# A gated mix of windowed attention and a ReGLU block with all its gradients: load order, a third unit of lag, one tensor for four gradients and outputs, and operand tiles for the first output group

## The chip, the cores and the metric

The kernel runs on one core of one Trainium2 chip. A core has TensorE (PE, the matrix products, with PEld as its weight loads), VectorE (DVE), ScalarE (ACT), GpSimd (POOL) and SyncE (SP), which here only issues DMAs. SP and ACT issue DMAs on queues of their own, and POOL on a third. The metric is the device time of one execution in microseconds (us), as the median of several runs. All engines run in program order and wait for each other by semaphores, so an instruction that waits holds up all that stand behind it on its engine.

## The reference

With x of 2048 rows and 512 columns in bf16, the forward part is

```
q, k, v = split(x @ wqkv)                  # 32 heads of 16
p = softmax(q k^T / 4, causal, window 256)
a = (p v) @ wo
b = (relu(x @ W_gate) * (x @ W_up)) @ W_down        # 1376 hidden columns
g = sigmoid(sum(x * gate_w))               # one number per row
out = g * a + (1 - g) * b
```

The kernel returns `out` and, for a given `grad_out`, the gradients of x, wqkv, wo, W_gate, W_up, W_down and gate_w: eight outputs in all.

## The kernel before

The names are those of the code. Rows come in 16 tiles of 128 (index t or j), which make 4 groups of 512 (TPG = 4 tiles, index tg); the 512 model columns are 4 chunks c of 128, that is 8 heads each; the 1376 hidden columns are 11 chunks fc.

**First loads (L143 to L163).** SP loads x for the first group, then the other three groups, then the first chunk of W_down (`Wd_sb`) and its rest. ACT's queue loads the first 256 columns of W_gate and W_up (`W0`), the gate vector as columns, and later the rest of both weights (L159, L160). POOL's queue loads grad_out by groups into `go_in`, which has two buffers: the third and fourth load are asked for in `db_rows` after the first and second group have been used.

**Feed-forward (L321 to L365).** A loop of steps n, one for each (fc, tg) pair, 44 in all. In step n the kernel does the gate and up products of pair n, in the first four steps also the transposes of x (`turn_x`), the gate column (`gate_col`), the rows (1-g)*grad_out (`db_rows`, on DVE) and one step later their transposes (`turn_db`). With a lag of 1 come the product `dh` and a DMA transpose of hT (`turn_h`), of 2 the DMA transpose of dgT, of 3 the transposes of duT on PE and the stores of hT, dgT and duT to DRAM (`keep`, on ACT's queue), of 4 the weight gradients (`weights`). Between them lie the rows g*grad_out (da), the zeroing of a DRAM scratch, and the load of wqkv and the transposed load of wo.

**Attention (L385 to L850).** `project_parts(c, tg)` makes Q, dO, K and V transposed for one chunk and group, then their rows. `spread` writes Q and dO to a DRAM scratch, `gather` reads them back in a block-diagonal tile `zt` (two of them, for two tiles j each), so that one product does four heads. A unit is (c, j, kb, half): one tile of queries, one of keys, four heads; there are 360, of role "d" (kb = j), "m" and "f". The hand-written order of one iteration n is: small POOL work that is due; `front` of unit n (ST and dPT on PE, exp on ACT, the mask on POOL); `gradp` of unit n-1 (DVE: Pd = Pu * dPT); `rowsum` and `flip` of unit n-2; one or two pieces of the CD products (the sums that give dK and dV); then background pieces (projections of the next group, or weight gradients of the chunk before, `grad_parts`); last the DMAs that are due. `flip` transposes Pu and Pd: for role "d" by a DMA on SP, for the others on PE with a copy on ACT or DVE in turn. `small_ops` divides by the row sums in five later iterations. PSUM has four banks of tag M (ST, dPT, projections and weight gradients), two of tag TR (transposes), one for CD and one for BA (row sums).

dQ, dK, dV (`dqkv_st`) and O (`O_st`) of a chunk stay in SBUF and are written by `spill`, half of the rows at a time, with four DMAs to two DRAM tensors: `dqkv_d`, where a row piece is 128 columns or 256 bytes, and `O_d`. The last half of the last chunk goes by POOL's queue.

During the last chunk `late_weights` (L478) loads the weights of the output stage on SP: wo, the transposed wqkv, W_gate and W_up from DRAM copies, and W_down, 5.9 MB, once the projections of the last group are done. `early_group` (L693) brings da rows and, from tile 12 on, the transposed dqkv and O of the first 256 rows. Behind the loop come `load_group(0)`, the 20 pieces of weight gradients of the last chunk, and their stores on SP from a tile `ws` with two buffers.

**Output stage (L872 to L934).** Eight groups of two tiles; while a group is computed the next is loaded on SP. A tile takes 11 products for b (`bps`), 4 for a (`aps`), the evictions and the gate's gradient dz on ACT, DVE and POOL, then 34 products for dx (`dxps`): the chunks of dgT and duT in turn, then 12 with dqT. The gate vector's gradient (`dgw_ps`) of a tile is added one tile later, and that of the last tile after everything else; its copy is on DVE. dx goes out on POOL's queue.

Of the kernel before, what the change touches and what calls it, by code (L numbers as in the profile page):

```python
# [22 lines left out]
def kernel(  # L23
# [64 lines left out]
    dqkv_d = dram.tile([S, 3 * D], BF, name="dqkv_d")  # L88
    O_d = dram.tile([S, D], BF, name="O_d")
# [33 lines left out]
    with ExitStack() as p1, tc.manual_schedule():  # L123
# [25 lines left out]
        nc.sync.dma_start(x_r[:, 0:TPG, :], rows_of(x_d, 0))  # L149
# [4 lines left out]
        load_go(0)  # L154
        load_go(1)
# [3 lines left out]
        nc.scalar.dma_start(Wg_sb[:, :, W0:F], Wg_v[:, :, W0:F])  # L159
        nc.scalar.dma_start(Wu_sb[:, :, W0:F], Wu_v[:, :, W0:F])  # L160
# [24 lines left out]
        def db_rows(tg):  # L185
            for k in range(TPG):
                t = tg * TPG + k
                nc.vector.tensor_scalar(db_r[:, t, :], go_in[tg][:, k, :], omg_all[:, t:t + 1], None, op0=ALU.mult)
            if tg + 2 < NTG:
                load_go(tg + 2)  # L190
# [81 lines left out]
        def turn_h(k):  # L272
            k.h_r = fp.tile([P, TPG, P], BF, tag="h_r", name="h_r")
            nc.sync.dma_start_transpose(out=k.h_r[:], in_=k.hT[:])
# [11 lines left out]
        def keep(k):  # L286
            for dst, src in ((hT_d, k.hT), (dgT_d, k.dgT), (duT_d, k.duT)):
                nc.scalar.dma_start(dst[k.fsl, k.ts], src[:])
# [31 lines left out]
        for n in range(N1 + 6):  # L320
# [16 lines left out]
            if at(2):  # L337
                turn_dg(at(2))
            if at(3):
                turn_du(at(3))  # L340
                keep(at(3))
            if at(4):
                f = weights(at(4))
# [24 lines left out]
    if True:  # L368
        st = p3.enter_context(tc.tile_pool(name="attst", bufs=2))
        gwp = p3.enter_context(tc.tile_pool(name="gwp", bufs=2))  # L370
        p3b = ExitStack()
        wq = p3b.enter_context(tc.tile_pool(name="wq", bufs=1))
# [3 lines left out]
        zt = [wq.tile([P, 2, HG, 2 * P], BF, name=f"z{i}") for i in range(ZB)]  # L376
# [8 lines left out]
        def project_parts(c, tg):  # L385
# [32 lines left out]
            def tr_kv():  # L418
# [3 lines left out]
                for a, lo, eng in ((0, 0, "dve"), (1, 17, "dve")):  # L422
# [3 lines left out]
            return [lambda: mm("Q", 0, "dve"), lambda: mm("dO", 3, "dve"), lambda: mm("K", 1, "dve"),  # L426
                    lambda: mm("V", 2, "dve"), tr_rows, tr_kv]
# [18 lines left out]
        def cd_piece(c, kb, qb, half, last):  # L446
# [12 lines left out]
            if last:  # L459
                nc.scalar.copy(sts[c][0][:, kb, 1:3, :].rearrange("p a (h d) -> p h a d", h=HG),  # L460
# [4 lines left out]
        def spill(c, t0):  # L465
            dqkv_st, O_st = sts[c]
            tsl = slice(t0, t0 + NT // 2)
            rsl = slice(t0 * P, (t0 + NT // 2) * P)
# [40 lines left out]
        def grad_parts(c, rest=None):  # L509
# [22 lines left out]
            def piece(part, t0, first, last):  # L532
                dqkv_st, O_st = sts[c]
                if first:
                    hold["w"] = ps.tile([P, 3, P] if part < DC else [P, D], F32, tag="M", bufs=4, name="wps")
                wps = hold["w"]
                for t in range(t0, t0 + 4):
                    go_, no_ = first and t == t0, last and t == t0 + 3
                    if part < DC:
                        nc.tensor.matmul(wps[:], lhsT=x_r[:, t, part * P:(part + 1) * P], rhs=dqkv_st[:, t, :, :],  # L540
                                         start=go_, stop=no_)
                    else:
                        nc.tensor.matmul(wps[:], lhsT=O_st[:, t, :], rhs=rows[t], start=go_, stop=no_)
                if not last:
                    return None
                if part < DC:
                    ws = gwp.tile([P, 3, P], BF, tag="ws", name="ws")
                    evac(ws[:], wps[:], "act")
# [7 lines left out]
                ws = gwp.tile([P, D], BF, tag="ws", name="ws")  # L556
# [8 lines left out]
            else:  # L565
                parts = [(p, 0, NT) for p in range(DC)] + [(DC, 0, NT)]
# [9 lines left out]
        for c in range(DC):  # L576
            for j in range(NT):
                kbs = [k for k in (j - 1, j, j - 2) if k >= 0]
                for half in range(2):
                    for ki, kb in enumerate(kbs):  # L580
# [4 lines left out]
                        u.role = ("d", "m", "f")[j - kb]  # L585
                        units.append(u)
        NU = len(units)

        def front(u):
            tg, jl = u.j // TPG, u.j % TPG  # L590
            zb = (jl // 2) % ZB
            KTt, VTt = proj[(u.c, u.kb // TPG)]["K"], proj[(u.c, u.kb // TPG)]["V"]
# [4 lines left out]
            u.dPT = ps.tile([P, HH, P], F32, tag="M", bufs=4, name="dPT")  # L597
            nc.tensor.matmul(u.dPT[:], lhsT=VTt[:, ksl], rhs=zt[zb][:, 1, hsl, (jl % 2) * P:(jl % 2 + 1) * P], start=True, stop=True)  # L598
# [3 lines left out]
            else:  # L602
                u.Pu = wk.tile([P, HH, P], BF, tag="Pu", bufs=3, name="Pu")
# [7 lines left out]

        def gradp(u):
            if u.role != "d":
                u.Pd = wk.tile([P, HH, P], BF, tag="Pd", bufs=3, name="Pd")
# [20 lines left out]
        def flip(u):  # L635
            if u.role == "d":
# [11 lines left out]
            p2 = wk.tile([P, 2, HH, P], BF, tag=f"P2{u.role}", bufs={"m": 6, "f": 4}[u.role], name="p2")  # L648
# [3 lines left out]
        def small_ops(c, j, s):  # L652
            rows = proj[(c, j // TPG)]["rows"]
            jl = j % TPG
            dqkv_st, O_st = sts[c]
# [18 lines left out]
            def pool2():  # L674
                nc.gpsimd.tensor_tensor(out=rq[:, :, Dh:2 * Dh], in0=hd(rows[:, 1, jl, :]),
                                        in1=bc(rinv[:], Dh), op=ALU.mult)
                nc.gpsimd.tensor_tensor(out=hd(O_st[:, j, :]), in0=BAs[:, :, 17:33], in1=bc(rinv[:], Dh), op=ALU.mult)
# [287 lines left out]
```

## Time and profile before

| | us |
|---|---|
| median of 3 runs | 1039.25 |
| lowest and highest | 1038.76, 1042.58 |
| the profiled execution | 1040.05 |
| its span in the profile | 1038.3 |
| PE busy | 982.8 (95%) |
| DVE busy | 569.8 (55%) |
| ACT busy | 481.1 (46%) |
| POOL busy | 466.4 (45%) |

The span is the profiled part of that one execution; 1.75 us lie around it. Busy time is the time in which an engine had an instruction of the kind that the profile counts; matmuls overlap and their ends are modelled, so the spacing of their starts says more than their durations. "PEclk" is the TensorE clock that was granted, in tenths. In the chain of waits each piece is the work or transfer that released the next one; a row reads start, length, what. In the timeline a row reads start, length, engine, line, operation, operands, count, and in brackets the idle time before it with what ended it. "SPq" and "ACTq" are the issuing of DMAs on these engines.

### The profile page before, as it was taken

To read this page: it belongs to the slowest core of one execution; us is meant where nothing else is said; L and a number is where in the kernel's file an instruction comes from. 1 tells how busy PE (TensorE), PEld (TensorE's weight loads), DVE (VectorE), ACT (ScalarE), POOL (GpSimd) and SP (SyncE) were. 2 spreads that over 40 slices of the span, in tenths; PEclk is the share of its full clock that TensorE was granted. 3 is DMA by queue.
4 is the path that set the end of the run, shared out by engine and by line. 5 is a ranking of instruction groups with operands and counts; after the bars stand their busy time and mean duration, and the time that the engine had idled before them with its cause. 6 is when DMAs were issued, how large, how long until landed. Compare 5 with 4: busy or idle time off the path is not lost.

```text
span 1038.3 us, 28954 instructions
## 1 busy us (share of the span) xinstructions
PE 982.8 (95%) x11852; PEld 634.0 (61%) x11852; DVE 569.8 (55%) x1101; ACT 481.1 (46%) x808; POOL 466.4 (45%) x810
## 2 busy tenths in 40 slices
PE   5799999999989999999999999999999769999997
PEld 3466666566647777677776777766777534444443
DVE  3344444333268888767788677886777502322222
ACT  3323333222147777666677676666667411001000
POOL 2355544344345556655556455565555411211211
PEclk9999999999999999999999999999999879999999
DMA  9557676866555676787767776569869989667740
GB/s 303 90 148 178 179 178 169 205 160 142 136 114 102 123 145 117 154 168 149 143 119 149 163 161 127 132 118 177 143 97 231 266 222 260 158 154 179 187 107 21
DMA packets 393335, 162.85 MB, mean 157 GB/s; under 512 B 293297, under 2 KB 388818, under 8 KB 393202
## 3 DMA queue, kind: packets, MB, share of 16 engines
q1 hardware_dynamic: 368306, 131.30, 60.6%
q10 hardware_dynamic: 21648, 20.13, 6.2%
q0 software_dynamic: 3248, 9.57, 3.0%
q8 instruction: 93, 1.52, 0.6%
q14 instruction: 40, 0.33, 0.1%
HBM read 54.36 MB, written 48.10 MB: 99 GB/s over the span
## 4 chain that ended last, share of the span: by engine, by line
PE 82%; DMA 7%; issue 3%; DVE 3%; ACT 2%; SPq 1%; POOL 1%; ACTq 0%; POOLq 0%; DVEq 0%
PE pt L647 9%; PE wps L298 7%; PE dPT L598 7%; PE ST L596 7%; PE gps L247 4%; PE bps L883 4%; PE dhps L247 4%; PE CD L454 4%; PE dxps L919 3%; PE BA L624 3%; PE dps L300 3%; PE pp L395 3%; PE ups L247 3%; PE dxps L912 3%; PE dxps L915 3%; PE wps L540 3%
## 5 line engine op out<-in xcount | busy, mean ns | idle before, releaser
L615 DVE TENSOR_TENSOR Pd<-Pu,dPT 128x512 bf16<-128x512 bf16 x232 | 158.3, 684 | 55.2 <-POOL Pu L609 34.1
L604 ACT ACTIVATE Pu<-ST 128x512 bf16<-128x512 f32 x232 | 139.5, 601 | 59.2 <-PE ST L596 53.2
L606 POOL TENSOR_SCALAR_AFFINE_SELECT PP<-PP 128x512 bf16<-128x512 bf16 x128 | 81.1, 634 | 160.7 <-ACT PP L604 160.1
L598 PE MATMUL dPT<-z,VT 128*128 128x512 bf16 x360 | 136.5, 379 | 4.1 <-DVE Pd L615 1.6
L596 PE MATMUL ST<-z,KT 128*128 128x512 bf16 x360 | 136.3, 379 | 0.8 <-DMA z<-z_d 0.8
L75 ACT COPY p<-pt 128x1024 bf16<-128x1024 bf16 x116 | 117.4, 1012 | 30.7 <-PE pt L647 30.3
L454 PE MATMUL CD<-rq,p 128*128 128x32 bf16 x1440 | 117.0, 177 | 7.9 <-DMA p<-PP 6.4
L457 PE MATMUL CD<-rq,p 128*128 128x16 bf16 x1440 | 113.7, 169 | 0.0
L261 POOL TENSOR_TENSOR hT<-rg,upm 128x512 bf16<-128x512 bf16 x44 | 50.5, 1148 | 134.5 <-DVE upm L259 114.0
L298 PE MATMUL wps<-dgu_r,x_r 128*128 128x256 bf16 x704 | 106.8, 275 | 2.1 <-DVE wst L77 2.0
L604 ACT ACTIVATE PP<-ST 128x512 bf16<-128x512 f32 x128 | 76.7, 600 | 55.0 <-PE ST L596 48.2
L454 PEld LDWEIGHTS <-p 128*128 128x128 bf16 x1440 | 95.8, 96 | 6.7 <-DMA p<-PP 6.7
L609 POOL TENSOR_SCALAR_AFFINE_SELECT Pu<-Pu 128x512 bf16<-128x512 bf16 x112 | 71.1, 634 | 56.3 <-ACT Pu L604 54.7
L77 DVE COPY p<-pt 128x1024 bf16<-128x1024 bf16 x116 | 79.7, 687 | 28.3 <-PE pt L647 26.8
L615 DVE TENSOR_TENSOR PP<-PP,dPT 128x512 bf16<-128x512 bf16 x128 | 86.6, 677 | 9.9 <-POOL PP L606 9.8
L624 PEld LDWEIGHTS <-Pu 128*128 128x128 bf16 x928 | 68.0, 96 | 37.3 <-issue 10.3
L647 PE MATMUL pt<-ident,Pd 128*128 128x128 bf16 x928 | 90.2, 220 | 0.0
L457 PEld LDWEIGHTS <-p 128*128 128x128 bf16 x1440 | 89.0, 96 | 1.7 <-issue 1.7
L647 PE MATMUL pt<-ident,Pu 128*128 128x128 bf16 x928 | 89.3, 218 | 0.0
L298 PEld LDWEIGHTS <-x_r 128*128 128x128 bf16 x704 | 67.6, 99 | 24.4 <-issue 3.2
L259 DVE SCALAR_TENSOR_TENSOR upm<-rg,ups 128x512 bf16<-128x512 bf16 x44 | 30.2, 687 | 94.0 <-PE ups L247 91.9
L624 PE MATMUL BA<-KV,Pu 128*128 128x33 bf16 x928 | 77.5, 178 | 4.5 <-ACT BAs L630 3.9
(136 smaller groups left out, 2073.8 us busy)
## 6 DMA issues: line engine op xcount, KB each, us to landing
z<-z_d SPq DMA_DIRECT2D x128, 64.0 KB
dar<-da_d SPq DMA_DIRECT2D x28, 256.0 KB
hT_d<-hT ACTq DMA_DIRECT2D x44, 128.0 KB
dgT_d<-dgT ACTq DMA_DIRECT2D x44, 128.0 KB
duT_d<-duT ACTq DMA_DIRECT2D x44, 128.0 KB
dqkv_d<-dqkv_st SPq DMA_DIRECT2D x21, 256.0 KB
hT_g<-hT_d SPq DMA_DIRECT2D x8, 640.0 KB
dgT_g<-dgT_d SPq DMA_DIRECT2D x8, 640.0 KB
```

The costliest lines, as they stand in the source:

```text
L75: nc.scalar.copy(out, in_)
L247: nc.tensor.matmul(out[:], lhsT=w(c), rhs=x(c), start=(c == 0), stop=(c == DC - 1))
L298: nc.tensor.matmul(acc["w"][:, c, :], lhsT=x_r[:, t, c * P:(c + 1) * P], rhs=k.dgu_r[:, :, i, :], start=(go_ and c % 2 == 0), stop=no_, sk ...
L454: nc.tensor.matmul(cd[0][:, h, :], lhsT=p2[:, 0, hh, :], rhs=rq[:, h, 0:2 * Dh], start=cd[1], stop=True, skip_group_check=True)
L457: nc.tensor.matmul(cd[0][:, h, 0:Dh], lhsT=p2[:, 1, hh, :], rhs=rq[:, h, 2 * Dh:3 * Dh], start=False, stop=True, skip_group_check=True)
L596: nc.tensor.matmul(ST[:], lhsT=KTt[:, ksl], rhs=zt[zb][:, 0, hsl, (jl % 2) * P:(jl % 2 + 1) * P], start=True, stop=True)
L598: nc.tensor.matmul(u.dPT[:], lhsT=VTt[:, ksl], rhs=zt[zb][:, 1, hsl, (jl % 2) * P:(jl % 2 + 1) * P], start=True, stop=True)
L604: nc.scalar.activation(u.Pu[:], ST[:], ACT.Exp, scale=scale)
L606: nc.gpsimd.affine_select(out=u.Pu[:], in_=u.Pu[:], compare_op=ALU.is_ge, fill=0.0, base=0, pattern=[[0, HH], [1, P]], channel_multiplier=-1)
L615: nc.vector.tensor_tensor(out=u.Pd[:], in0=u.Pu[:], in1=u.dPT[:], op=ALU.mult)
L624: nc.tensor.matmul(BA[:, h, 0:33], lhsT=u.Pu[:, hh, :], rhs=kv[:, u.kb % TPG, h, :], start=(u.first and hh == 0), stop=True, skip_group_ch ...
L647: nc.tensor.transpose(pt[:, a, hh, :], src[:, hh, :], ident[:])
```

## The change

*First loads.* x of the first group comes in two halves. go_in has four buffers and all four loads are asked for at the start. The rest of W_gate and W_up moves from ACT's queue to SP's, behind x and the first chunk of W_down and ahead of its rest. A sigmoid on one zeroed column is put at the front of ACT's work. Every second row of `db_rows` goes to ACT. `dh` runs two steps behind instead of one, `turn_dg` three, `turn_du` four, `weights` five; `keep` stores hT at a lag of 3 and the other two at 4. `h_r` has six buffers.

*Attention.* `rowsum` and the flips on PE run three units behind (LAG), the DMA flips still two. `front` is split: ST and the exp stay, dPT moves to `front_dp`, behind the row sums and flips. Pu and Pd outside the diagonal have four buffers, P2m five. K and V are copied by ACT. In the prelude the first spreads and gathers are written ahead of K and V.

*One tensor.* dQ, dK, dV and O lie side by side in one SBUF tile `rows_st` and one DRAM tensor `dqkvo_d`, by chunk, so that a spill is one DMA with runs of 1 KB and a group's transposed load is one DMA.

*End of attention.* The last projections are due 10 iterations sooner, and `late_weights` with them. The diagonal units of the last two tiles of the last chunk are flipped on PE. hT and dgT of the first output group are loaded into the two `zt` tiles when their last readers are done, and the first group's transposes start from tile 11. Of the last chunk's weight gradients, 12 pieces are done two at a time in the last iterations, in four M banks; then come four for wo's gradient and the last four. `ws` has five buffers there, and its copies alternate between ACT and DVE. The tiles of later groups share `rows_st`.

*Output stage.* dxps takes all chunks of dgT, then all of duT, then dq. In the last tile both dgw products come ahead of the dq products, the copy is on ACT, and the last dx goes out on SP.

```diff
-            go_in[tg] = fp.tile([P, TPG, D], BF, tag="go_in", bufs=2, name="go_in")
+            go_in[tg] = fp.tile([P, TPG, D], BF, tag="go_in", bufs=NTG, name="go_in")
...
+        half = TPG // 2
+        for i in range(2):
+            nc.sync.dma_start(x_r[:, i * half:(i + 1) * half, :], rows_of(x_d, 0)[:, i * half:(i + 1) * half, :])
...
+        nc.vector.memset(g_all[:, 0:1], 0.0)
+        nc.scalar.activation(g_all[:, 0:1], g_all[:, 0:1], ACT.Sigmoid)
...
-        nc.scalar.dma_start(Wg_sb[:, :, W0:F], Wg_v[:, :, W0:F])
-        nc.scalar.dma_start(Wu_sb[:, :, W0:F], Wu_v[:, :, W0:F])
+        nc.sync.dma_start(Wg_sb[:, :, W0:F], Wg_v[:, :, W0:F])
+        nc.sync.dma_start(Wu_sb[:, :, W0:F], Wu_v[:, :, W0:F])
...
+                if k % 2:
+                    nc.scalar.mul(db_r[:, t, :], go_in[tg][:, k, :], omg_all[:, t:t + 1])
...
+            if at(2):
+                dh(at(2))
             if at(1):
-                dh(at(1))
                 turn_h(at(1))
...
-            for a in range(3):
-                eng.dma_start(dqkv_d[rsl, a * D + c * P:a * D + (c + 1) * P].rearrange("(t p) n -> p t n", p=P),
-                                  dqkv_st[:, tsl, a, :])
-            eng.dma_start(O_d[rsl, c * P:(c + 1) * P].rearrange("(t p) n -> p t n", p=P), O_st[:, tsl, :])
+            eng.dma_start(dqkvo_d[t0 * P:(t0 + NT // 2) * P, c * 4 * P:(c + 1) * 4 * P].rearrange("(t p) n -> p t n", p=P),
+                          sts[c][:, tsl, :, :].rearrange("p t a n -> p t (a n)"))
...
-                parts = [(p, 0, NT) for p in range(DC)] + [(DC, 0, NT)]
+                for a, b in ((0, NT - 4), (NT - 4, NT)):
+                    if a:
+                        out += [(DC, t0, t0 == 0, t0 + 4 == NT) for t0 in range(0, NT, 4)]
+                    out += [(p, t0, t0 == 0, t0 + 4 == NT) for p in range(DC) for t0 in range(a, b, 4)]
+                return [lambda a=a: piece(*a) for a in out]
...
+                        u.dma = u.role == "d" and (c < DC - 1 or j < NT - 2)
...
+        def early_f(i):
+            flat = wq.tile([P, 2, HG, 2 * P], BF, tag=f"z{i}", name=f"f{i}")[:].rearrange("p a h q -> p (a h q)")
+            S2[f"f{i}"] = flat[:, 0:FC * GT * P].rearrange("p (c s) -> p c s", c=FC)
+            load_f(S2[f"f{i}"], (hT_d, dgT_d)[i], slice(0, GT * P))
...
+                            if gi + 2 == len(groups):
+                                due -= 10
...
-                if 2 <= n < NU + 2:
-                    w = units[n - 2]
+                if 2 <= n < NU + 2 and units[n - 2].dma:
+                    flip(units[n - 2])
+                if LAG <= n < NU + LAG:
+                    w = units[n - LAG]
                     rowsum(w)
-                    flip(w)
+                    if not w.dma:
+                        flip(w)
...
+                if u is not None:
+                    front_dp(u)
...
+                    elif n > NU + 1:
+                        for _ in range(2):
+                            if len(S2["grads"]) > 4 + DC:
+                                S2["grads"].pop(0)()
```

More of the change, by code (lines that the diff above doesn't have):

```diff
@@ L284, in turn_du, with keep @@
             evac(k.dgu_r[:, 1, :, :], pt[:], "dve")
-        def keep(k):
-            for dst, src in ((hT_d, k.hT), (dgT_d, k.dgT), (duT_d, k.duT)):
+        def keep(k, *pairs):
+            for dst, src in pairs:
                 nc.scalar.dma_start(dst[k.fsl, k.ts], src[:])
@@ L319 @@
         stores = {}
-        for n in range(N1 + 6):
+        for n in range(N1 + 7):
             at = lambda lag: steps[n - lag] if 0 <= n - lag < N1 else None
@@ L375 @@
         ZB = 2
-        zt = [wq.tile([P, 2, HG, 2 * P], BF, name=f"z{i}") for i in range(ZB)]
+        zt = [wq.tile([P, 2, HG, 2 * P], BF, tag=f"z{i}", name=f"z{i}") for i in range(ZB)]
         for i in range(ZB):
@@ L532, in piece @@
             def piece(part, t0, first, last):
-                dqkv_st, O_st = sts[c]
                 if first:
-                    hold["w"] = ps.tile([P, 3, P] if part < DC else [P, D], F32, tag="M", bufs=4, name="wps")
-                wps = hold["w"]
+                    tag, bufs = ("TR", 2) if part == DC and rest is not None else ("M", 4)
+                    hold[part] = ps.tile([P, 3, P] if part < DC else [P, D], F32, tag=tag, bufs=bufs, name="wps")
+                wps = hold[part]
                 for t in range(t0, t0 + 4):
@@ L734, in load_group @@
-            return hT_g, dgT_g, duT_g, dqT_g, go_g, OT_g
+                T_g, hT_g, dgT_g = S2["T0"], S2["f0"], S2["f1"]
+                go_g = S2["g6"].tile([P, GT, D], BF, tag="go_g", bufs=1)
+            else:
+                flat = st.tile([P, NT, 4, P], BF, tag="rows_st", name="gt")[:].rearrange("p t a n -> p (t a n)")
+                n1, n2 = 4 * DC * GT * P, (4 * DC + FC) * GT * P
+                T_g = flat[:, 0:n1].rearrange("p (c s) -> p c s", c=4 * DC)
+                hT_g = flat[:, n1:n2].rearrange("p (c s) -> p c s", c=FC)
+                go_g = flat[:, n2:n2 + GT * D].rearrange("p (t d) -> p t d", t=GT)
+                dgT_g = S2["g6"].tile([P, FC, GT * P], BF, tag="dgT_g")
+                load_f(hT_g, hT_d, gsl)
@@ L736 @@
+            duT_g = S2["g6"].tile([P, FC, GT * P], BF, tag="duT_g")
+            nc.sync.dma_start(go_g[:] if g == 0 else go_g, go_d[gsl, :].rearrange("(t p) d -> p t d", p=P))
+            if g > 0:
+                load_f(dgT_g, dgT_d, gsl)
+            load_f(duT_g, duT_d, gsl)
+            if g > 0:
+                nc.sync.dma_start_transpose(out=T_g, in_=dqkvo_d[gsl, :])
+            return hT_g, dgT_g, duT_g, T_g, go_g
         groups = [(c, tg) for c in range(DC) for tg in range(NTG)]
         with tc.manual_schedule():
[L738 removed]
+            parts = project_parts(*groups[0])
@@ L739 @@
+            for f in parts[:2]:
                 f()
@@ L854 @@
             grp_next = load_group(0)
-            for f, more in S2["grads"]:
+            for f in S2["grads"]:
                 store = f()
@@ L872 @@
             for g in range(NG):
-                hT_g, dgT_g, duT_g, dqT_g, go_g, OT_g = grp_next
+                hT_g, dgT_g, duT_g, T_g, go_g = grp_next
                 if g + 1 < NG:
@@ L924 @@
                         nc.tensor.matmul(dgw_ps[:], lhsT=pdz[:], rhs=x_r5[:, pt_, :], start=(pt_ == 0), stop=False)
+                    if t == NT - 1:
+                        nc.tensor.matmul(dgw_ps[:], lhsT=dz_bf[:], rhs=x_r5[:, t, :], start=False, stop=True)
+                        dgw_sb = t6.tile([1, D], BF, tag="dgw_sb")
+                        nc.scalar.copy(dgw_sb[:], dgw_ps[:])
+                        nc.sync.dma_start(out_7.rearrange("(o d) -> o d", o=1), dgw_sb[:])
                     pending_dgw = (t, dz_bf)
+                    for cc in range(C3):
+                        nc.tensor.matmul(dxps[:], lhsT=T_g[:, 4 * (cc % DC) + cc // DC, lsl], rhs=wqkvT_sb[:, cc, :],
+                                         start=(i == 0), stop=(i == nmm - 1))
+                        i += 1
                     dx_sb = t6.tile([P, D], BF, tag="dx_sb")
```

155 lines of the change are left out of this document (68 added, 87 removed).

## The prediction

> **What bounds the kernel now.** I read the page's slices first: they show where TensorE is not full.
>
> ```profile
> span 1038.3 us, 28954 instructions
> PE   5799999999989999999999999999999769999997
> PEclk9999999999999999999999999999999879999999
> DMA  9557676866555676787767776569869989667740
> PE 82%; DMA 7%; issue 3%; DVE 3%; ACT 2%; SPq 1%; POOL 1%; ACTq 0%; POOLq 0%; DVEq 0%
> ```
>
> A slice is 26 us. PE is full except in the first two, around slices 31 to 33 and in the last, and the chain that ended last is 82% PE. So a microsecond counts only where PE stands. The table of windows over the stages gives the amounts (length, then busy time of PE, PEld, DVE, ACT, POOL, then granted clock, DMA share, GB/s):
>
> ```profile
> 0.00:50.00 50.00, 30.07 (x282) 19.43 (x283) 18.53 (x39) 17.85 (x25) 16.21 (x20) 0.97 0.78 203
> 200.00:210.00 10.00, 7.98 (x49) 4.75 (x47) 3.87 (x6) 2.54 (x5) 3.53 (x4) 0.86 1.09 254
> 284.00:300.00 16.00, 12.04 (x80) 5.82 (x81) 11.00 (x20) 3.57 (x6) 4.98 (x6) 1.00 0.29 79
> 300.00:350.00 50.00, 46.78 (x821) 33.59 (x819) 39.88 (x80) 36.95 (x61) 30.85 (x66) 1.00 0.67 118
> 350.00:800.00 450.00, 446.19 (x7710) 325.26 (x7707) 343.76 (x672) 313.29 (x526) 252.75 (x538) 1.00 0.74 145
> 800.00:856.00 56.00, 40.48 (x566) 27.37 (x565) 17.09 (x34) 19.21 (x35) 19.04 (x39) 0.82 1.03 241
> 856.00:1031.00 175.00, 175.00 (x798) 76.34 (x796) 49.24 (x110) 18.79 (x32) 36.06 (x47) 1.00 0.62 158
> 1031.00:1039.00 8.00, 0.60 (x3) 0.09 (x2) 1.34 (x2) 0.00 (x0) 0.58 (x1) 0.85 0.05 17
> ```
>
> PE idles 19.9 us in the head, 2.0 at 200, 4.0 where the feed-forward part ends, 3.2 + 3.8 in all of attention, 15.5 around attention's end, and nothing in the output stage. Only head and end can give much.
>
> **The head.** From the chain of waits, in order of time, and the waits of SP's own queue:
>
> ```profile
> 6.22 2.24 ACTq L160
> 8.49 1.28 ACT L75
> 10.85 1.86 PE gps L247 x4
> 15.49 1.28 ACT L182
> 19.40 11.78 DMA go_in<-in_grad_out_dram
> 33.07 1.89 PE dhps L247 x4
> 50.56 0.86 PE gps L247 x4
> 55.98 0.86 PE gps L247 x4
> SPq L161 <- DMA Wu_sb<-in_B_W_up_dram: 6.4, 1, 6.4
> ```
>
> ACT stood in issuing a late weight load (L160), loaded its table only then, and PE's first product waited for ACT's copy. A second table load followed for the sigmoid. The third go_in was asked for at 19.40, when a buffer came free, and took 11.78 us; the DVE products, the transposes and dhps stood behind it. The last row shows that a load on one queue can wait for one on another.
>
> The change takes both W rests off ACT, loads the table once during the x load, asks for all go_in at once and moves dh one step later, so that dh no longer stands directly behind its transposes. PE starts about 2.2 earlier (the L160 row), at 8.7. Then I lay PE's steps end to end: a product of four is 0.86 (row 50.56), four transposes 0.22 (below), so turn_x or turn_db is 0.88; the gate column is 0.54:
>
> ```profile
> 20.38 0.54 PE L179 MATMUL zps<-gw_col,x_T 128*128 128x1 bf16 x16
> ```
>
> Step 0 is two products, turn_x, gate column, turn_wd: 3.4, and as products run at half rate at first (1.86 against 0.86) about 5.4, to 14.1. Step 1 (no dh yet) 4.0, step 2 4.9, step 3 4.0, step 4 3.9: 30.9. Step 5 is a full one of 5.42 (50.56 to 55.98): 36.3. Of it gate and up (1.72) are beyond what before had done at 50.56, so the comparable point is 34.6: 16 earlier. That supposes that data is there: x, the first W columns, go and the first Wd are 4.7 MB, the head's row moves 203 GB/s on average, and Wd's rest now stands on SP behind both W rests (2.3 MB) while step 4 needs it near 30 us. ACT's store of hT, issued in step 3, can wait for such a load as SP did, with ACT's evictions behind it. I take 4 off: **12**. Ends: 3.5 (the L160 row and one table load, 2.24 + 1.28) and 16. The POOL issues lie ahead of POOL's first work. The ACT share of db_rows (eight, priced at the 0.69 of DVE's copy further below) lies in idle time, ACT being busy 17.85 of 50; were that cover gone, it would cost 5.5.
>
> The Trainium skill ("ScalarE: Activation LUTs", What ACT_TABLE_LOAD costs) counts a drain of about 1380 ns with each switch of tables, 2.66 us in total; the row at 15.49 has 1.28 and the chain shows no drain beside it, so the measurement decides; by the page the sum would be 1.4 better.
>
> **Feed-forward.** At 200 the chain has
>
> ```profile
> 199.17 6.39 DMA hT_d<-hT
> ```
>
> ACT's queue waiting for a store while wqkv and woT load. One step more before the weight gradients, and hT stored a step ahead of the other two, soften it; the stores stay on ACT. I take **1**, of 0 to 2. The lag adds no instruction. Where attention begins (4.0 idle), spreads and gathers are on SP and the projections on PE, DVE and ACT, so emitting them in another order changes no engine's order: **0**; K and V on ACT could help or hurt by 1.
>
> **Attention.** One unit on PE in the timeline (start, duration):
>
> ```profile
> 503.64 0.38 PE L596 MATMUL ST<-z,KT 128*128 128x512 bf16 x1
> 504.07 0.18 PE L624 MATMUL BA<-KV,Pu 128*128 128x33 bf16 x1
> 504.27 0.38 PE L647 MATMUL pt<-ident,Pu 128*128 128x128 bf16 x4
> 504.71 0.18 PE L454 MATMUL CD<-rq,p 128*128 128x32 bf16 x1
> 504.92 0.38 PE L596 MATMUL ST<-z,KT 128*128 128x512 bf16 x1
> ```
>
> A unit is 1.28 back to back: ST and dPT 0.43, row sums 0.20, flips 0.44, CD 0.21. The number of matmuls stays, so only the 7.0 of idle can go, and stalls hidden in the modelled ends, some 3 more by my estimate (PE's steps added up at their spacing in this unit fall that much short of the stage). Row sums three behind leave the Pd product one unit more, and dPT behind them holds its PSUM buffer for a shorter time. I take **5**, of 0 to 10. K and V add 32 evictions to ACT (313 busy of 450) and take them from DVE (344): hidden.
>
> **End of attention.** The chain:
>
> ```profile
> 806.81 15.22 DMA p<-PP x2
> 825.99 6.83 DMA p<-PP
> 833.32 4.76 DMA p<-PP
> 843.90 3.58 SPq L728
> 847.52 4.90 DMA out_dram<-ws
> 855.80 2.54 PE bps L883 x11
> ```
>
> DMA transposes of diagonal blocks lie on SP behind 5.9 MB of late weights; then the stores of ws lie behind 2.3 MB of group 0 and hold ws's two buffers. The change flips the last four diagonal units on PE (4 x 0.44 = 1.8 more, and four copies on ACT and DVE, idle there), starts the late weights up to 10 units (12.8) sooner, puts hT and dgT of group 0 into freed z tiles, fills PE with 12 gradient pieces between the last CD products, and gives ws five buffers. A spill becomes one DMA with runs of 1 KB for four with 256 B, so eight issues for 32; SP has fewer to issue ahead of the gathers. New waits: dgT's load waits for the last reads of z, with go_g and duT queued behind it on SP; duT is read only after bps, aps and the dg products, some 5.7 (26 products at 0.22). Group 1's hT waits for the last spill, and its data has two tiles' time, 22. Both are covered. Of the 15.5 idle 1.8 goes to the flips and some 2.7 to CD's evictions and transposes that still queue: **11**. Ends: 3.4 (the rival below) and 18, all idle and the half clock (0.82 in that row) gone. Had SP's earlier weights no free DMA time, the flips and fills would have nothing to fill and the low end holds.
>
> **Output stage and tail.** PE is full and keeps its count: 0. In the last tile:
>
> ```profile
> 1028.32 2.75 PE L919 MATMUL dxps<-wqkvT_sb,dqT_g 128*128 128x512 bf16 x12
> 1028.74 0.16 DVE L906 CAST dz_bf<-dz 128x1 bf16<-128x1 f32 x1
> 1031.12 0.75 DVE L927 SCALAR_TENSOR_TENSOR dx_sb<-gw_b,dz,dxps 128x512 bf16<-128x512 bf16 x1 [2.21 <-PE dxps L919]
> ```
>
> The last dgw product now stands ahead of these 12 and waits for dz_bf, ready at 1028.9, when PE gets there at 1028.5 (after the dgw product of the tile before): some 0.4, plus 0.43 for two dgw products, so dx comes 0.8 later. In return its store goes by SP, not POOL, and dgw is out early. I call it **0**, between 1 worse and 1 better.
>
> Sum: 12 + 1 + 0 + 5 + 11 + 0 = 29. The profiled execution took 1040.05 (its span and 1.75 around it): 1011; the median of before is 0.8 below it: **1010**.
>
> **Rivals.** *Transfers bind as before.* In the head everything asked for at once shares the same engines, and only 3.5 goes. At the end DMA is busy (1.03) in the whole row; if the same bytes must land, 12.8 us of earlier start in time 0.74 busy yields 12.8 x 0.26 = 3.4. With 5 in attention the gain is 12: 1027. For it: both rows. Against: in the head the loads that PE needs first are put first, and 1 KB runs and four transposes less lighten the end. The Trainium skill ("DMA: Bandwidth & Descriptors", Issuing engines are not separate DMA queues) says that issuing from more engines saves only sequencer time, which is this rival's ground; the two DMA shares agree.
>
> *Slower: dPT comes late.* It is now issued about 0.64 (row sums and flips) after ST, and DVE's Pd follows. Such a wait stands in DVE's timeline, with the copies that DVE makes:
>
> ```profile
> 796.44 0.69 DVE L615 TENSOR_TENSOR Pd<-Pu,dPT 128x512 bf16<-128x512 bf16 x1 [0.62 <-PE dPT L598]
> L77 DVE COPY p<-pt 128x1024 bf16<-128x1024 bf16 x116 | 79.7, 687 | 28.3 <-PE pt L647 26.8
> ```
>
> In a unit where DVE also copies a flip it has 0.69 + 0.69 for 1.28, no room. If each of these 116 loses 0.62, that is 72: 1082. From 0.25 each it eats all 29. Against it: the extra unit of lag, 1.28, is twice 0.62.
>
> *The lag does nothing, or all.* The waits that end last in attention may be others: 5 worse, 1015; all 10 found: 1005. Both lie in the forecast's range.
>
> **Chances.** The forecast, 998 to 1020: 0.70. Transfers bind, to 1034: 0.18. Slower by dPT: 0.06. The rest 0.06, mostly head or end alone cancelled by small losses. A measurement tells 0.5%, 5.2 us, from no change. Faster by more: 0.70 + 0.18 + 0.01 = 0.89; within: 0.05; slower: 0.06. The range, 998 to 1028, holds the forecast and takes in most of the rival of the transfers; all low ends together (5 gained) would be 1034, all high ones (48 gained) 991.
>
> **What would show it.** Right: gps near 8.7, one table load ahead of it, no go_in and no p<-PP in the chain, bps starting some 29 before 855.80, idle in 350 to 800 near 1 to 2. Wrong: dhps or ptw still behind a load after 20 us; PE idle at the end with DMA share 1; DVE's Pd waiting for dPT all through attention; bps behind duT or ws.

## The result: 2.8% faster, and where the time went

The changed kernel takes 1011.61 us (median of 4 runs, 1009.29 to 1012.23) against 1039.15 for the kernel before (median of 4 runs beside it). The ratio is 0.9724, with a 95% interval of 0.9698 to 0.9750. The profiled execution of the changed kernel was the shortest of its four, with a span of 1007.6, so the spans differ by 30.7 and the medians by 27.5.

The page of the changed kernel, its span, its slices and its chain by engine:

```profile
span 1007.6 us, 28956 instructions
PE   5999999999989999999999999999999899999998
PEclk9999999999999999999999999999999899999999
DMA  9658678975466677777766786668759997766650
PE 88%; DMA 5%; issue 2%; ACT 2%; SPq 1%; DVE 1%; POOL 1%; POOLq 0%; ACTq 0%; DVEq 0%
```

The dip of PE at slices 31 to 33 is nearly gone, the first slice is as empty as it was, and the chain is 88% PE in place of 82%. The table of windows (length, then busy time of PE, PEld, DVE, ACT, POOL, then granted clock, DMA share, GB/s):

```profile
0.00:42.00 42.00, 30.73 (x294) 20.00 (x295) 18.81 (x33) 21.53 (x34) 17.16 (x21) 1.00 0.85 251
180.00:190.00 10.00, 10.00 (x69) 6.14 (x67) 2.91 (x5) 1.32 (x3) 4.41 (x4) 1.00 1.20 231
331.00:772.00 441.00, 437.34 (x7580) 321.25 (x7577) 316.37 (x637) 321.32 (x542) 250.27 (x530) 1.00 0.72 147
772.00:828.00 56.00, 50.01 (x820) 36.57 (x818) 27.37 (x55) 29.94 (x51) 22.96 (x48) 0.94 1.14 267
828.00:1003.00 175.00, 174.83 (x797) 76.10 (x795) 49.27 (x110) 19.40 (x33) 36.08 (x47) 1.00 0.60 151
```

The head still idles 11.3 us and the end of attention 6.0; the stall of the feed-forward part is gone although the DMA share there is 1.20. In the long attention row PE is idle for 3.7 of 441, about as much as before (3.8 of 450), so what attention gained is not to be seen in this column.

The chain of waits of the changed kernel up to the output stage, its pieces of 3.5 us and more that are not PE (and the first product of that stage):

```profile
0.81 3.91 DMA Wg_sb<-in_B_W_gate_dram
4.73 13.03 DMA Wd_sb<-in_B_W_down_dram
264.69 4.81 issue
286.04 5.14 DMA p<-PP
416.31 5.60 DMA dar<-da_d
686.33 4.49 DMA dar<-da_d
781.57 7.93 DMA z<-z_d
827.67 2.54 PE bps L920 x11
```

No go_in is in it and, at the end, no p<-PP; a load of z stands there instead. Markers that both kernels have let the gain be followed through the span. The first is the gate product that follows the first weight gradients; this row is from the timeline of the kernel before, then four of the changed one's head:

```profile
50.39 0.38 PE L247 MATMUL gps<-x_T,Wg_sb 128*128 128x512 bf16 x1
```

```profile
7.69 1.87 PE L251 MATMUL gps<-x_T,Wg_sb 128*128 128x512 bf16 x4 [1.10 <-ACT x_T L75]
12.81 1.89 PE L174 MATMUL ptx<-ident,x_r 128*128 128x128 bf16 x16 [3.25 <-DMA x_r<-in_A_x_dram]
17.81 0.40 PE L228 MATMUL ptw<-ident,Wd_sb 128*128 128x128 bf16 x4 [1.01 <-DMA Wd_sb<-in_B_W_down_dram]
41.68 1.03 PE L251 MATMUL gps<-x_T,Wg_sb 128*128 128x512 bf16 x4
```

With the lag the changed kernel has done one more gate and up pair at that point (1.72), so 39.96 compares with 50.39. The other markers: the chain's piece of 4.81 that closes the feed-forward part (278.98 before), the first and the 330th ST, the first bps, the end of the span.

| marker | before | changed | gain so far | of this stage | forecast |
|---|---|---|---|---|---|
| gate product after the first weights | 50.39 | 39.96 | 10.4 | 10.4 | 12 |
| end of feed-forward | 278.98 | 264.69 | 14.3 | 3.9 | 1 |
| first ST | 295.65 | 281.23 | 14.4 | 0.1 | 0 |
| 330th ST | 777.97 | 759.91 | 18.1 | 3.6 | 5 |
| first bps | 855.80 | 827.67 | 28.1 | 10.1 | 11 |
| end of the span | 1038.3 | 1007.6 | 30.7 | 2.6 | 0 |

Every term lies within its ends, except the feed-forward's (3.9, of 0 to 2) and the tail's (2.6, of -1 to 1). But these are single traces, and that of the changed kernel is its shortest execution. In a second trace of it (`changed_again`, below) the gains by stage are 8.5, 3.9, 0.1, 0.6, 9.7 and 2.6, together 25.3: the head and attention vary by 2 and 3 us from one execution to the next. Whether the parts earned what they were credited with is another question, which the experiments answer in part.

### The profile page after: what moved, and what is told of

Same layout as the page of the kernel before. It is cut to its first block, busy times and chain, and to the rows that moved or that the text cites. A ratio compares the mean times of both kernels' runs of the same rounds, so it can differ in the third digit from the quotient of the medians.

```text
span 1007.6 us, 28956 instructions
## 1 busy us (share of the span) xinstructions
PE 975.8 (97%) x11884; PEld 635.4 (63%) x11884; DVE 543.6 (54%) x1065; ACT 503.8 (50%) x849; POOL 464.0 (46%) x806
## 2 busy tenths in 40 slices
DMA packets 367110, 161.79 MB, mean 161 GB/s; under 512 B 259809, under 2 KB 362626, under 8 KB 366978
## 4 chain that ended last, share of the span: by engine, by line
PE 88%; DMA 5%; issue 2%; ACT 2%; SPq 1%; DVE 1%; POOL 1%; POOLq 0%; ACTq 0%; DVEq 0%
PE pt L661 10%; PE ST L603 7%; PE wps L302 7%; PE dPT L624 7%; PE dxps L950 7%; PE wps L542 4%; PE dxps L963 4%; PE BA L638 4%; PE CD L460 4%; PE pp L401 4%; PE dps L304 4%; PE bps L920 4%; PE ups L251 4%; PE dhps L251 4%; PE gps L251 3%; PE CD L463 2%
## 5 line engine op out<-in xcount | busy, mean ns | idle before, releaser
L629 DVE TENSOR_TENSOR Pd<-Pu,dPT 128x512 bf16<-128x512 bf16 x232 | 155.9, 682 | 23.2 <-PE dPT L624 10.5
L75 ACT COPY p<-pt 128x1024 bf16<-128x1024 bf16 x118 | 119.5, 1013 | 8.7 <-PE pt L661 3.9
L463 PEld LDWEIGHTS <-p 128*128 128x128 bf16 x1440 | 88.9, 96 | 41.0 <-issue 1.3
L460 PEld LDWEIGHTS <-p 128*128 128x128 bf16 x1440 | 104.2, 96 | 0.4 <-issue 0.2
L927 ACT COPY a_sb<-aps 128x512 f32<-128x512 f32 x16 | 9.4, 586 | 150.5 <-issue 137.6
```

Of the source, the lines that this page charges most:

```text
L75: nc.scalar.copy(out, in_)
L460: nc.tensor.matmul(cd[0][:, h, :], lhsT=p2[:, 0, hh, :], rhs=rq[:, h, 0:2 * Dh], start=cd[1], stop=True, skip_group_check=True)
L463: nc.tensor.matmul(cd[0][:, h, 0:Dh], lhsT=p2[:, 1, hh, :], rhs=rq[:, h, 2 * Dh:3 * Dh], start=False, stop=True, skip_group_check=True)
L629: nc.vector.tensor_tensor(out=u.Pd[:], in0=u.Pu[:], in1=u.dPT[:], op=ALU.mult)
```

## The experiments

Twelve kernels ran, in three groups with the kernel before beside each on its chip; the ratios are to that. For single traces "the attention" is the time from the first to the 330th ST (482.3 before, 478.7 changed) and "the end" from there to the first bps (77.8 and 67.8). Two traces of the changed kernel give a first idea of the scatter: 478.7 and 481.7 for the attention, 67.8 and 68.2 for the end. The other kernels widen it. The eight traces with the changed attention code have 477.9 to 481.7 (mean 479.3), the four with that of before 482.1 to 482.7 (mean 482.4). Two kernels with the same code at the end, `weights_after_gather` and `in_turn_after_gather`, have 64.2 and 68.6 there.

### The head: loads or lag

The theory was that the order of the loads carries the head. Its rival gives the lag the larger part. Three kernels are the kernel before with one of the two edits, or both.

`head_loads`, the loads alone (in words where there is no code):

```
+ go_in: bufs=NTG, all four loads at the start
+ early Sigmoid; odd rows of db_rows on ACT
- nc.scalar.dma_start(Wg_sb[:, :, W0:F], ...)   # and Wu_sb
+ nc.sync.dma_start(Wg_sb[:, :, W0:F], ...)
```

> The kernel before with the change's order of loads alone: four buffers of go, the weight remainders on SP, the early Sigmoid, half of db_r on ACT; dh is still one step behind and keep is one piece. Theory (the loads carry the head, the lag carries the stall at 200): the gain of 10.4 at the fifth step is there almost whole, 8 to 11, and the 2.0 us stall at 200 stays, so 1028 to 1031. Rival (the loads only uncover waits of dh for its operands, and the lag is what lets them pay): under 5 gained, 1034 or above, and PE's waits in the first 60 us are at L262 and at the transposes of dg and du.

`head_lag`, the lag alone (shortened; h_r also gets its six buffers):

```
- if at(1): dh(at(1)); turn_h(at(1))
- if at(2): turn_dg(at(2))
- if at(3): turn_du(at(3)); keep(at(3))
- if at(4): f = weights(at(4))
+ if at(2): dh(at(2))
+ if at(1): turn_h(at(1))
+ if at(3): turn_dg(at(3)); keep(hT)
+ if at(4): turn_du(at(4)); keep(dgT, duT)
+ if at(5): f = weights(at(5))
```

> The kernel before with the change's lags alone: dh two steps behind, h, dg, du and the weight gradients one step later, keep in two pieces, six buffers of h_r; the loads are as before. Theory: the loads bind the first 50 us as before, and only the stall at 200 (2.0 us and the slow clock after it) and a little of the other waits go: 2 to 5 gained, 1034 to 1037. Rival (the lag carries the head as well): 8 or more gained, 1031 or below. Second rival (the lag only shifts the work, nothing gained): 1038 to 1040.

`head_both` has both:

> The kernel before with both edits of the feed-forward stage and nothing of the attention or the end. Theory: the 14.3 us that the markers show up to the last dps come whole and nothing later changes: 1024 to 1026. It also tests whether the parts add: if loads alone and lag alone sum to clearly more or less than this, one covers for the other.

| kernel | us | ratio, interval | gain at the first marker | gain at the end of feed-forward |
|---|---|---|---|---|
| head_loads | 1035.55 | 0.9975, 0.9959 to 0.9991 | 0.6 | 2.0 |
| head_lag | 1027.88 | 0.9896, 0.9863 to 0.9928 | 5.6 | 9.0 |
| head_both | 1025.01 | 0.9869, 0.9837 to 0.9901 | 10.4 | 14.2 |

The theory fell. Six rows of PE's timeline with the loads alone show why (the last is the first marker), and its chain still has the stall at 200:

```profile
26.08 1.02 PE L252 MATMUL dhps<-db_T,WdT 128*128 128x512 bf16 x4 [1.90 <-ACT db_T L75]
32.91 1.02 PE L252 MATMUL dhps<-db_T,WdT 128*128 128x512 bf16 x4 [1.90 <-ACT db_T L75]
38.85 1.72 PE L252 MATMUL dhps<-db_T,WdT 128*128 128x512 bf16 x4 [1.89 <-ACT db_T L75]
40.79 1.85 PE L252 MATMUL gps<-x_T,Wg_sb 128*128 128x512 bf16 x4
46.11 1.02 PE L252 MATMUL dhps<-db_T,WdT 128*128 128x512 bf16 x4 [1.10 <-ACT db_T L75]
49.80 1.03 PE L252 MATMUL gps<-x_T,Wg_sb 128*128 128x512 bf16 x4
```

```profile
198.58 6.71 DMA hT_d<-hT
```

The data is there early, but in every step of the start dhps stands directly behind the transposes of its own db, and so behind the gate column, the sigmoid, db_rows, the transposes and their eviction. It waits 1.90, 1.90, 1.89 and 1.10, and behind the third of these waits products run at half rate (1.72 and 1.85 in place of 1.02). What the loads won, this chain of small steps took back. With the lag alone the waits of dhps are gone and that for one late load, the third go_in, is left (its row in PE's timeline, and the marker):

```profile
33.34 1.69 PE L198 MATMUL ptd<-ident,db_r 128*128 128x128 bf16 x16 [3.48 <-DVE db_T L77]
46.50 1.03 PE L247 MATMUL gps<-x_T,Wg_sb 128*128 128x512 bf16 x4
```

By the traces the two edits give 0.6 + 5.6 = 6.2 apart and 10.4 together. Some 2.0 of the difference is not theirs: in the trace with the loads alone the products between 18 and 22 us ran at half rate, and the gate column of step 1 came at 22.73 against 20.72 with both edits, before any wait of dhps. Such a slow start comes and goes between executions (next section). The rest fits the reading that each edit leaves in place a wait that the other removes, but the medians do not show a surplus: 0.25% and 1.04% make 1.29%, beside 1.31% for both. What stands is the order: the loads alone give little, the lag alone most. The stall at 200 goes with the lag: with both edits PE is busy in all of the 30 us that hold it, at a DMA share of 1.00.

```profile
180.00:210.00 30.00, 30.00 (x205) 18.82 (x203) 11.48 (x18) 7.48 (x14) 14.27 (x12) 1.00 1.00 215
```

So the lag edit, with hT stored a step ahead of the other two and one step more before the weight gradients, takes ACT's queue out of the way; which of the two does it was not run apart. The feed-forward's 3.9 is that stall with the clock behind it: in the kernel before PE idled 2.0 us there, and the granted clock was 0.86 in the row at 200. With the loads alone the idle time is 2.3 but the clock stayed at 1.00, which fits the 1.4 that this kernel gains in the stretch with the stall in place.

### The head again: the order of need

The changed head still had PE waiting 3.25 for x and 1.01 for the first Wd (rows above). `in_turn_after_gather` asks only for the first go on POOL and puts SP's loads in the order of need; it also has the gather's edit of the section below.

```
- for tg in range(NTG): load_go(tg)              # all on POOL
- SP: x1, x2, x3, Wd chunk 0, W rests, Wd rest
+ load_go(0)                                     # POOL
+ SP: x1, Wd chunk 0, go1, x2, go2, x3, go3, W rests, Wd rest
```

> The changed kernel with the WuT load behind the last gather of z, and with another order of the first loads: the second go on SP and no longer all four at once on POOL, and the SP queue in the order of need (x of group 0, x of group 1, the first chunk of Wd, then go and x of groups 1, 2, 3 in turn, then the weight remainders). Theory (between 10 and 18 us PE waits for x of group 1, 3.25, and for the first chunk of Wd, 1.01, because four loads of go share the DMA engines with them): 3 to 4 from the head and 2 to 4 from the gather, 1004 to 1007. Rival (the same bytes must land before step 2 whatever their order): the head's fifth step starts within 1 of where it is, and only the gather's part is left, 1007 to 1010.

`changed_again` is the changed kernel on the same chip:

> The changed kernel itself, once more, to stand on the same chip beside the three kernels below: 1008 to 1013. Nothing is decided by it alone.

It took 1010.46 (ratio 0.9722, 0.9700 to 0.9744), and `in_turn_after_gather` 1006.87 (0.9683, 0.9665 to 0.9700). PE's timeline of the latter:

```profile
10.03 1.89 PE L175 MATMUL ptx<-ident,x_r 128*128 128x128 bf16 x16 [0.39 <-DMA x_r<-in_A_x_dram]
13.35 0.38 PE L229 MATMUL ptw<-ident,Wd_sb 128*128 128x128 bf16 x4
38.21 1.03 PE L252 MATMUL gps<-x_T,Wg_sb 128*128 128x512 bf16 x4
```

The waits are 0.39 and none, and the marker comes 3.5 before that of the changed kernel's first trace. The end is 68.6, as long as in the changed kernel, so by the traces the 3.6 in the medians is the head's, and the gather's edit gave none of the 2 to 4 that its theory had.

The rows of `changed_again` show that the same head can cost 2 us more:

```profile
18.09 0.40 PE L228 MATMUL ptw<-ident,Wd_sb 128*128 128x128 bf16 x4 [1.75 <-DMA Wd_sb<-in_B_W_down_dram]
19.50 1.91 PE L174 MATMUL ptx<-ident,x_r 128*128 128x128 bf16 x16
43.63 1.03 PE L251 MATMUL gps<-x_T,Wg_sb 128*128 128x512 bf16 x4
```

Here the wait for Wd is 0.74 longer, the transposes behind it run at half rate (1.91 against 1.06), and the marker is at 43.63 against 41.68. The length of the wait does not decide it: in the trace of `weights_later` the same wait is 1.54 and the transposes take 1.06, in that of `f_late` it is 0.76 and they take 1.88. Of the ten traces with this head, six reach the first ST at 281.1 to 281.7 and four at 282.9 to 283.4. The Trainium skill ("TensorE: Matmul & The Clock Gate", What's actually happening) says that PE reaches its full clock only after a window of sustained work, that the window runs free, and that equal kernels therefore differ at the start; the traces agree.

### Attention: the third unit of lag, and the joined spills

`sums_two_behind` sets `LAG = 2`:

> The changed kernel with the row sums two units behind in place of three. Theory (the forecast's attention term: the lag removes the waits of p for P, worth most of the 3.6 gained in attention): 2 to 4 slower than the changed kernel, 1013 to 1016, with p<-PP waits back in 350 to 770. Rival (the fewer table and copy steps carry the gain, and the lag is cover that nothing needs): within 1 of it. Second rival (two is better, since the third unit holds a buffer longer): over 1 faster.

`spill_four` writes the joined tensor with four DMAs of 256-byte runs:

> The changed kernel with each spill of the joined tensor as four transfers of 256-byte runs, as before the change, in place of one of 1 KB runs. Theory (the spills lie far ahead of their readers, in the middle of the attention stage, and only packets change): within 1 of the changed kernel, with about 25000 packets more. Rival (small packets crowd the queue and hold up da_d and z): 2 to 4 slower, with longer waits for z and dar in the attention stage.

| kernel | us | ratio, interval | attention |
|---|---|---|---|
| sums_two_behind | 1012.89 | 0.9752, 0.9738 to 0.9767 | 484.1 |
| spill_four | 1012.28 | 0.9739, 0.9720 to 0.9757 | 482.6 |

With two units the attention is 2.4 to 5.4 longer than in the two traces of the changed kernel, and longer than in any of the eight traces above. The median ratio is 0.3% above 0.9724, though the intervals overlap. A part is lost again: with two units the end is 65.7, 2.1 to 2.5 shorter, and ST waits 2.56 there for z in place of 4.43 (below). What the lag does is plain in the groups of DVE's Pd product (busy and mean ns of one, then the idle time before it and what ended it). In order: before, two units behind, changed:

```profile
L615 DVE TENSOR_TENSOR Pd<-Pu,dPT 128x512 bf16<-128x512 bf16 x232 | 158.3, 684 | 55.2 <-POOL Pu L609 34.1 <-ACT Pu L604 14.8 <-PE dPT L598 5.0
```

```profile
L629 DVE TENSOR_TENSOR Pd<-Pu,dPT 128x512 bf16<-128x512 bf16 x232 | 158.9, 685 | 67.1 <-POOL Pu L614 44.2 <-ACT Pu L609 12.6 <-PE BA L640 3.9
```

```profile
L629 DVE TENSOR_TENSOR Pd<-Pu,dPT 128x512 bf16<-128x512 bf16 x232 | 155.9, 682 | 23.2 <-PE dPT L624 10.5 <-POOL Pu L614 8.1 <-ACT Pu L609 1.8
```

With three units Pd hardly waits for the mask on POOL, 8.1 in place of 44.2. The later dPT costs 10.5 of DVE's idle time in all, 0.05 for each of 232 products, where the rival that forecast a slower kernel had 0.62 in 116, 72 in all.

The spills are inconclusive: the trace's attention is 1 to 4 longer than the two of the changed kernel (0.9 above the longest of the eight), but the ratio is only 0.15% higher and the intervals overlap for the most part. Packets went from 367110 to 388998.

### The end of attention: five parts, one of them a loss

`grads_behind` keeps the last gradient pieces behind the loop (`> 4 + DC` becomes `> 20`):

> The changed kernel with the last group's gradient pieces held until the unit loop has ended, as before the change, in place of being dealt among the last CD products. Theory (the forecast's end term: pieces among the products fill PE's waits, while behind the loop they stand alone): 3 to 6 slower, 1015 to 1018, with PE idle again in the last units. Rival (PE is dense at the end since the operands of group 0 come from one tensor and early, not through the dealing): within 1 of the changed kernel.

`f_late` loads hT and dgT of the first output group in `load_group(0)`, not while units still run:

> The changed kernel with hT and dgT of the first group loaded with the rest of that group, when the output stage starts, in place of early into the tiles of z. Theory (the end term is the early operands: 15 us of end chain were loads and their stores): bps starts later by 4 to 9 and the kernel takes 1015 to 1021, with PE idle ahead of bps and the DMA share near 1. Rival (the load is hidden under the gradient pieces anyway): within 1.

`dma_flips_tail_pool` turns the last four diagonal units by DMA again (`u.dma = u.role == "d"`), and stores the last dx from POOL:

> The changed kernel with two parts undone that lie 180 us apart and are read from the start of the first bps: the last four diagonal units are turned by DMA transposes again, and the last rows of dx are stored from POOL. Theory for the flips (the 15.22 us wait for p in the chain of before was those transposes behind the late weights): bps starts 3 to 7 later. Rival for the flips (the early weights have already cleared SP's queue): within 1. Theory for the store (the way of a store of POOL costs the end 3 to 4 us): from bps to the end 2 to 4 longer. Rival for the store (it was the late dgw that closed the kernel before): within 0.5. In sum 1016 to 1021 by both theories, 1010 to 1013 by both rivals.

`weights_later` drops two lines, `if gi + 2 == len(groups): due -= 10`:

> The changed kernel with the late weights let go ten units later, as before the change. Theory (the earlier start of 5.9 MB on a DMA that is 0.74 busy there yields 12.8 x 0.26 = 3.3 by the forecast's working): bps starts 2 to 5 later, 1014 to 1017. Rival (with the diagonal blocks turned on PE nothing in the last units is behind those loads any more): within 1 of the changed kernel. Second rival (later is better, as the gather of z then finds the queue free): the wait of ST for z at 789.63 is gone and bps starts earlier by 1 to 4.

`weights_after_gather` lets each late load go one unit later, which puts WuT's behind the last gather of z (`n % 5 == 2` becomes `n % 5 == 3`):

> The changed kernel with the late loads of turned weights let go at n % 5 == 3 in place of 2, so that the load of WuT lies behind the last gather of z on SP's queue and not ahead of it. Theory: the 4.43 us wait of ST for z at 789.63 and the slow clock behind it come from that load alone: 4 to 6 faster than the changed kernel, 1005 to 1008. Rival (the gather is late because the scattered z itself is late): within 1 of the changed kernel, and the wait stands where it was. Second rival (the load is then late for its own use at the start of the output stage): the ST wait is gone and as much is lost ahead of bps.

| kernel | us | ratio, interval | end | what the part was worth there |
|---|---|---|---|---|
| grads_behind | 1013.51 | 0.9765, 0.9737 to 0.9792 | 71.9 | 3.7 to 4.1 gained by the dealing in the trace |
| f_late | 1010.24 | 0.9726, 0.9711 to 0.9741 | 67.4 | nothing |
| dma_flips_tail_pool | 1016.54 | 0.9768, 0.9750 to 0.9785 | 69.3 | 1.1 to 1.5 gained by the flips on PE in the trace, within the scatter |
| weights_later | 1004.36 | 0.9660, 0.9643 to 0.9678 | 61.8 | **6.0 to 6.4 lost** by the early weights |
| weights_after_gather | 1009.42 | 0.9722, 0.9688 to 0.9756 | 64.2 | 3.6 in the trace, none in the median |

In the trace the dealing is worth what its theory said, and the ratio without it is 0.4% higher, though the intervals overlap. Without it the chain runs through the pieces one behind the other once the last CD is done:

```profile
814.99 9.70 PE wps L542 x48
824.70 3.45 PE wps L545 x16
828.15 2.61 PE wps L542 x16
831.32 2.54 PE bps L920 x11
```

The kernel with the DMA flips also stores from POOL. Its median is 6.1 above that of `changed_again` on the same chip, and the intervals do not touch; the store is 3.3 of it ("The tail", below), which leaves some 2.8 to the flips and to chance.

The surprise is `weights_later`. Its interval and that of `changed_again`, from the same chip, do not touch: the part of the change that starts the late weights ten units sooner costs 6.1 us of median. (The two lines also move the last transposes of the last projections, from 750.09 to 763.63. The products before them and the stores of z stay where they were: the first store is issued at 742.92 and 742.60. No run moves the weights without these transposes.) SP's own timeline in the changed kernel shows how, with the product of PE that waits:

```profile
767.55 2.98 SPq L494 DMA_DIRECT2D WgT_sb<-WgT_d  x1
778.94 0.74 SPq L492 DMA_DIRECT2D WuT_sb<-WuT_d  x1
779.73 1.17 SPq L494 DMA_DIRECT2D WuT_sb<-WuT_d  x1
780.94 2.50 SPq L442 DMA_DIRECT2D z<-z_d  x4
789.63 0.59 PE L603 MATMUL ST<-z,KT 128*128 128x512 bf16 x1 [4.43 <-DMA z<-z_d]
```

and with the weights let go later:

```profile
775.40 3.52 SPq L442 DMA_DIRECT2D z<-z_d  x4
785.74 1.38 SPq L494 DMA_DIRECT2D WgT_sb<-WgT_d  x1
```

The last gather of z is issued 5.5 us later when it lies behind WgT and WuT on SP, and then shares the DMA engines with WuT: it takes 7.93 in the chain, ST waits 4.43 us for it, and PE comes back at half rate (a granted clock of 0.50 from 789.6 to 793 and 0.77 in the 4 us after that). Let go later, the weights land in time all the same: bps waits 0.57 for ACT in both kernels and for no load. PE is busy 59.3 of the last 62 us at a DMA share of 1.04, and the only long wait left in the chain is a diagonal block:

```profile
760.00:822.00 62.00, 59.32 (x1024) 44.28 (x1024) 35.90 (x73) 37.76 (x63) 30.29 (x64) 1.00 1.04 258
```

```profile
798.65 7.18 DMA p<-PP
822.00 2.54 PE bps L918 x11
```

It isn't enough to move WuT alone. In the trace of `weights_after_gather` ST no longer waits for z, but two waits for p<-PP, 6.53 and 8.11, are in the chain; that trace is the shortest of five runs (1005.38, the others 1008.73 to 1010.56), and the median shows no gain. The second kernel with this edit, `in_turn_after_gather`, has a wait for p of 8.41 and the full end. So it seems that the weights as a whole crowd that stretch, and not WuT alone.

The four parts that were undone one at a time sum to about -1 (4 + 1.3 + 0 - 6.2), and the end gained 10. The rest lies with what wasn't tried (five buffers for ws, the transposes from the joined tensor, the PE flips together with later weights) or with parts that cover for each other, so that undoing one alone shows little. Each may clear the queue of transposes that held the kernel before for 15.22 us. Which it is stays open.

### The tail

The store of the last dx is read in the same kernel. The last two rows of the timeline with POOL's store (span 1015.4), then of `changed_again` with SP's (span 1013.0):

```profile
1008.51 0.75 DVE L967 SCALAR_TENSOR_TENSOR dx_sb<-gw_b,dz,dxps 128x512 bf16<-128x512 bf16 x1 [3.17 <-PE dxps L963]
1009.55 0.58 POOL L969 DMA_DIRECT2D out_dram<-dx_sb  x1 [5.32 <-DVE dx_sb L967]
```

```profile
1009.44 0.75 DVE L967 SCALAR_TENSOR_TENSOR dx_sb<-gw_b,dz,dxps 128x512 bf16<-128x512 bf16 x1 [3.17 <-PE dxps L963]
1010.22 0.36 SPq L969 DMA_DIRECT2D out_dram<-dx_sb  x1
```

From the start of the DVE product to the end of the span it is 6.9 with POOL and 3.6 with SP: the queue of the last store is worth 3.3, and all of the difference from the first bps to the end (183.2 against 179.9). The order of dgw has no part in that. Other traces bear it out: the same stretch is 3.4 to 3.8 in the eight others that store from SP, and 7.1 in the four that have the tail of before, with POOL's store and the late dgw.

## Why the prediction held, and where its working didn't

- **The time**: 1010 forecast, 1011.61 measured. The sum of 29 stands beside 30.7 in the profiled spans, 25.3 with the second trace, and 27.5 in the medians. That the sum is so near owes something to luck: its errors in the feed-forward, the tail and within the end cancel with those in the head and attention.
- **The head, 12**: 10.4, and gps at 7.69 (8.7 forecast) behind one table load. The term priced loads and lag as one, and as one it holds. Its low end of 3.5, from the issue row and a table load, was taken from the loads alone, which gave 0.6 at the marker (2.6 but for the slow start of that execution). The working laid the steps end to end; 4 were taken off for data that is late, and the waits for x at 12.81 (3.25) and for the first Wd at 17.81 (1.01) are about that much. The two other delays that it feared did little: ptw at 33.44 has no wait for Wd's rest, and PE's waits after 20 us are 0.94 for DVE and 0.46 for ACT.
- **Feed-forward, 1**: mis-sized, 3.9. "Soften it" was too little: the stall went whole, with the slow clock behind it, which the sum did not price.
- **Transition, 0**: 0.1.
- **Attention, 5**: 3.6 in one trace and 0.6 in the other, 3.1 between the means above. The lag took away the wait that was named, Pd behind POOL's mask and ACT, and with two units in place of three the gain is gone from the trace. That PE's idle time would fall to 1 or 2 was wrong: it stayed near 3.7. What went may lie in stalls hidden in the modelled ends, of which the working had "some 3 more"; no view shows them.
- **End, 11**: 10.1, right in sum, by luck in part, and wrong in a step. The start of the late weights "up to 10 units (12.8) sooner" was counted as a gain, 3.4 by the rival's own formula. It cost 6, so the other parts earned some 16 if the parts add, and the experiments account for about 5 of that. The step that failed is that it looked at the DMA engines' free share and not at what else is queued on SP there: the gather of z, which is on the same queue. "New waits" listed the loads behind dgT and group 1's hT, not this one. (By their shapes the late weights are 6.3 MB, not 5.9; no term uses it.)
- **Tail, 0**: 2.6. dx comes 1.0 later (176.3 after the first bps, 175.3 before), as the forecast's 0.8 has it; "its store goes by SP, not POOL" was named and, with dgw's earlier store, taken for 1 at most; it measured 3.3.
- **Rivals**: the transfers do not hold the gain to 3.5 in the head and 3.4 at the end, though PE did wait for x behind the four loads of go. The late dPT is there, with 10.5 of DVE's idle time where 72 were priced and 29 would have eaten the gain.

## What to carry to other kernels

A load that comes earlier pays only if the first consumer isn't the last link of a chain within its own step; try the lag and the load order together, and each alone. One trace of each is not enough for gains of 2 or 3 us, as the start alone varies by 2. Before moving bulk loads forward, list what is queued behind them on the issuing engine and when PE needs it: free DMA share doesn't price that. The changed kernel without its two lines for early weights took 1004.36, less than either; with the loads in order of need as well it might be some 3.6 lower by the head's part, which was not run.

## What was not expected of the hardware

- The last store of the kernel costs 3.3 us more from POOL than from SP, between two traces that otherwise agree from the first bps to the last dx product (176.33 in both).
- The same code's head differs by 2 us from one execution to the next, with half rate for some 3 us. The wait for Wd ahead of it does not decide it: half rate came behind waits of 0.76 and 1.75, full rate behind 1.01 and 1.54.
- A wait of PE for a load counts more than its own length: 4.43 us for z in the changed kernel, and behind it a granted clock of 0.50 for 3.4 us and 0.77 for 4. At these shares some 2.6 us of work is lost, an estimate; together that is 7.0, where the end grew 6.0 to 6.4 shorter when the wait went.
